# Attention with a routed expert layer: block table 0 emitted with preference, expert chunks let in earlier

## The chip, the cores and the metric

The kernel runs on one core of one Trainium2 chip. Its work is spread over TensorE (PE in the profile, with its weight loads as a row PEld of their own), VectorE (DVE), ScalarE (ACT), GpSimd (POOL) and the DMA queues, of which SyncE (SP) issues most. The metric is device time in microseconds (us) of one execution. Before the change three runs took 975.03, 975.57 and 981.8 us, with a median of 975.57 us; lower is better.

## The reference

An attention over 8 batches and 8 heads of 576 tokens and 64 dimensions, in which scores that are more than `tau` under the maximum of their row are left out, feeds a layer of 8 experts; each token goes to the one expert with the highest gate logit.

```python
scores = scale * np.matmul(q, k.transpose(0, 1, 3, 2))
thresh = np.max(scores, axis=-1, keepdims=True) - tau
scores = np.where(scores >= thresh, scores, -1000000000.0)
attn = np.exp(scores - np.max(scores, axis=-1, keepdims=True))
attn_out = np.matmul(attn / (np.sum(attn, axis=-1, keepdims=True) + 1e-09), v)
x = attn_out.transpose(0, 2, 1, 3).reshape(B * S, H * D)      # 4608 x 512
logits = x @ w_gate
expert_idx = np.argmax(logits, axis=1)
gate_w = softmax(logits)[np.arange(N), expert_idx]
for e in range(E):                                            # 8 experts
    mask = expert_idx == e
    out[mask] = gate_w[mask, None] * (np.maximum(x[mask] @ w1[e], 0.0) @ w2[e])
```

## The kernel before, in words

**Attention.** The 64 heads go in 32 pairs, 0 to 31, four pairs to a batch (called a block here, 0 to 7). The main loop goes through steps k, 11 to a pair; the attention's last step is 351 and `KEND` is 352. In a step the kernel emits one tile of `s` (scores from which DVE takes the row maxima, L358 to L370) for a pair ahead, and one tile of `st` (transposed scores less the threshold, L406 and L407) for the current pair. An `st` tile passes ACT (`exp`, L423) and DVE (mask, L426); of each two tiles ACT then makes an f16 copy `ph` (L431) and POOL the rest `pl` (L432). From `ph` and `pl` PE forms the product with the values (`av`, L476), some steps later. `st_30_1` is tile 1 of pair 30; `e_30_0`, `ph_30_0` and `pl_30_0` hold tiles 0 and 1 of it. Tiles `s`, `st`, `hi` and the experts' `h` all live in one pool of six PSUM banks (`ps_sc`).

**Routing.** When a block's four pairs are done, `finish` (L510) divides, splits and transposes its rows (transposes issued by SP, L552), `logits` (L560) forms gate logits `lg` on PE (L570), `route` (L585) takes the largest on DVE and ranks the tokens with a few matmuls `rk` (L621 to L624), and each token's row is sent to its expert's place in `xs` in DRAM (L644, POOL).

**Tables.** An expert's rows are read back in slots of 128. Which rows a slot holds stands in a table, made by `level` (L1018) from the counts (`pc`, L674) on DVE. Table 0 (`row0`, from `tables0`) is made after block 5 and serves slots 0 to 2, table 1 after block 6 and serves slots 3 to 6, table 2 after block 7 and serves the others. `fetch` (L830) gathers a slot's rows with POOL (L858, into `Rm`) and has SP transpose them into `xTm` (L868).

**Experts.** `gemm1` (L889, matmuls `h` of L913) and `gemm2` (L925, `y` of L946) are generators that hand their work over in chunks, 12 matmuls of 128 columns or the like each. The main loop lets chunks in by `RATE`: none before step `KM`, a fraction of a chunk a step from there to `KEND`, one a step after it.

**Order.** The order in which the program emits instructions is a preference. A scheduler places them on each engine by that preference and by when it expects operands and buffers to be ready; `hurry` (L181) marks what is emitted in it as preferred. Once placed, the order on each engine is fixed.

Of the kernel before, what the change touches and what calls it, by code (L numbers as in the profile page):

```python
# [26 lines left out]
EARLY = ((3, 0), (4, 3))  # L27
# [15 lines left out]
CAP = NTOK  # L43

TUNE = dict(
    lead=10, cast=2, sl=8, ll=15, sp0=3, sps=0, lv=-16, sv0=-6, sv1=2, av=2, g=4, l=3, d=4, g5=4, l5=3, d5=2, g6=1, l6=2, d6=2, g7=1, l7=1, d7=1, off=2, off5=1, off6=5, lg=4, lg7=6, km=16, rate=15, dh=1, do=3, ws0=6, wsd=2, w1d=5, plv=1, xv=5, so=0, sto=0, ord=0, sc=6, fa=3, fd=4, wa1=-70, wa2=-86, wl1=-28, wl2=-6, avb=1, route=1, ranks=7, pp=8, ew=4, maskat=0, w1a=-40, w1b=3,
)


# [1 line left out]
def kernel(  # L51
# [19 lines left out]
    ew = ctx.enter_context(tc.tile_pool(name="ew", bufs=4))  # L71
# [8 lines left out]
    pp = apool.enter_context(tc.tile_pool(name="pp", bufs=8))  # L80
# [100 lines left out]
    def hurry(f):  # L181

        def g():
            was, urgent[0] = urgent[0], True
            with tc.high_priority():
                f()
            urgent[0] = was

        return g

    def after(k, f, where=END):
        plan(now[0] + k, f, where)
# [479 lines left out]
    def counts(nm):  # L672
        pc = ps_m.tile([P, 512], F32, tag="m", name=f"pc_{nm}")
        nc.tensor.matmul(pc[:, 0:E], ones, run, start=True, stop=True)  # L674
        c = tp.tile([P, E], F32, name=f"cnt_{nm}")
        nc.vector.tensor_tensor(c, pc[:, 0:E], base_e, ALU.subtract)
        return c, pc

    def table_first(nm, bank, cnt, start=None):

        bc = [P, E, NE]
        if start is None:
            rk_i = tp.tile(bc, I32, name="rk_i")
            nc.gpsimd.iota(rk_i, pattern=[[0, E], [P, NE]], base=0, channel_multiplier=1)
            nc.vector.tensor_copy(rk_f, rk_i)
        rk, bad = (bank[:, z:z + E * NE].rearrange("p (e n) -> p e n", e=E) for z in (32, 96))
        if start is None:
            nc.scalar.copy(rk, rk_f)
        else:
            nc.vector.tensor_tensor(rk, rk_f, start.unsqueeze(2).to_broadcast(bc), ALU.add)  # L690
        lim = tp.tile([P, E, 1], F32, name=f"lim{nm}")
        nc.vector.scalar_tensor_tensor(lim[:, :, 0], bank[:, 0:E], -1.0, base_e, ALU.add, ALU.subtract)
        nc.vector.tensor_tensor(bad, rk, lim.to_broadcast(bc), ALU.is_gt)
        nc.vector.tensor_scalar(bad, bad, float(1 << 20), None, ALU.mult)
        badi = to_int(bad, bc, f"badi{nm}")
        nc.vector.tensor_tensor(rk, rk, lim.to_broadcast(bc), ALU.min)
        nc.vector.tensor_tensor(rk, rk, base_e.unsqueeze(2).to_broadcast(bc), ALU.add)

        has = tp.tile([P, E, 1], F32, name=f"has{nm}")
        nc.vector.scalar_tensor_tensor(has[:, :, 0], bank[:, 0:E], -0.5, base_e, ALU.add, ALU.is_gt)  # L700
        nc.vector.scalar_tensor_tensor(rk, rk, pos0, has.to_broadcast(bc), ALU.subtract, ALU.mult)
        nc.vector.tensor_scalar(rk, rk, pos0, None, ALU.add)
        rowi = to_int(rk, bc, f"row{nm}")
        return rowi, badi
# [81 lines left out]
    T = {}  # L786
# [231 lines left out]
    def level(nm, n, prev):  # L1018

        (cnt, bank), s_e, sp = counts(nm), None, None  # L1020
        if prev:

            nbe = tp.tile([P, E], F32, name=f"nbe{nm}")
            nc.vector.memset(nbe, 0.0)
            for e, i in enumerate(n[0]):
                if i:
                    nc.vector.memset(nbe[:, e:e + 1], float(i * P))
            s_e = tp.tile([P, E], F32, name=f"s_e{nm}")
            sp = bank[:, 16:16 + E]
            if prev[1] is None:  # L1030
                nc.scalar.copy(sp, prev[0])
                nc.vector.tensor_tensor(sp, sp, nbe, ALU.min)
            else:
                nc.scalar.copy(sp, prev[1])
                nc.vector.tensor_tensor(sp, sp, nbe, ALU.add)
                nc.vector.tensor_tensor(sp, sp, prev[0], ALU.min)
            nc.vector.tensor_tensor(sp, sp, nbe, ALU.subtract)
            nc.scalar.copy(s_e, sp)
        row, bad = table_first(nm, bank, cnt, sp)
        for e in range(E):  # L1040
            a, z = (x[e] if e < len(x) else 0 for x in n) if n[1] else (n[0][e] if e < len(n[0]) else 0, NE)
            for i in range(a, z):
                slots[NE * e + i] = row[:, e, i:i + 1], bad[:, e, i:i + 1], e % 2
                placed[NE * e + i] = B - 3 + int(nm)
        return cnt, s_e

    def tables0():
        T[0] = level("0", ((), EARLY[0]), None)
        for m in range(NF):
            after(1 + m, lambda m=m: fetch(m))  # L1050

# [44 lines left out]
    for i in range(8):  # L1096
        plan(k + WS0 + WSD * i, lambda i=i: split_w(*wseq[i]))
        if i + 2 < 8:
            plan(k + WS0 + WSD * i, lambda i=i: load_w(*wseq[i + 2]))
    TABLES = {B - 3: tables0, B - 2: tables1, B - 1: tables2}  # L1100
    plan(KEND + 12, close)

# [206 lines left out]
```

## Time and profile before

| what | value |
|---|---|
| median of the three runs | 975.57 us |
| the profiled execution's own time | 974.36 us |
| its span, first to last instruction | 972.6 us |
| PE busy | 932.8 us, 96% |
| PEld busy | 604.0 us, 62% |
| DVE busy | 696.2 us, 72% |
| ACT busy | 652.7 us, 67% |
| POOL busy | 559.0 us, 57% |
| HBM traffic | 90.24 MB read, 19.44 MB written |

Matmuls are pipelined: each row lasts until its result is out, while the next one starts long before that, so 96% of busy PE does not say that PE had no room. The shares are of the whole span; they change between the attention (to about 570 us, with three of the other engines near full) and the experts (from there on, with PE alone near full).

### The profile page before, as it was taken

Reading aid. Unit: us, or ns where it says so; the run is one execution under the profiler, and the core shown is the slowest. Engines: PE = TensorE matmul, PEld = TensorE weight load, DVE = VectorE, ACT = ScalarE, POOL = GpSimd, SP = SyncE. Lnnn points to the kernel's source line nnn. Section 1 sums busy time; section 2 is a strip of 40 time slices with the busy share of each in tenths; the row PEclk is TensorE's granted clock in tenths of the full one; section 3 lists DMA queues with packets and bytes.
Section 4 is the critical chain, followed back from the end, with each engine's and each line's share of the span. In section 5 each row is a group of like instructions: output and inputs, shape, how many; then the busy total and the mean of one; then the engine's idle time right before and its main releaser. Section 6 shows DMA issues by size and latency. Waiting matters only on the chain. (4 is left out here: it accounts for less than half of the span.)

```text
span 972.6 us, 28577 instructions
## 1 busy us (share of the span) xinstructions
PE 932.8 (96%) x11548; PEld 604.0 (62%) x11548; DVE 696.2 (72%) x1413; ACT 652.7 (67%) x1111; POOL 559.0 (57%) x467
## 2 busy tenths in 40 slices
PE   7899999999999999999997989999999999999997
PEld 2355555556556556565664677776677666677684
DVE  8899999999989999999999756835243341432650
ACT  2789898998988998989889944435333342433651
POOL 6466887897977998869979851531221212221121
PEclk9899999999999999999999999999999999999999
DMA  7642555474654674654647569998475565656720
GB/s 202 185 135 73 142 137 143 93 196 123 130 161 134 162 147 134 176 146 104 154 133 207 95 168 304 396 234 212 127 231 157 166 177 155 206 143 209 219 103 28
DMA packets 142707, 159.19 MB, mean 164 GB/s; under 512 B 96361, under 2 KB 112747, under 8 KB 142572
## 3 DMA queue, kind: packets, MB, share of 16 engines
q1 hardware_dynamic: 125782, 100.03, 41.1%
q10 hardware_dynamic: 7638, 27.85, 9.2%
q0 software_dynamic: 9152, 29.45, 8.9%
q8 instruction: 92, 1.51, 0.7%
q14 instruction: 43, 0.35, 0.1%
HBM read 90.24 MB, written 19.44 MB: 113 GB/s over the span
## 5 line engine op out<-in xcount | busy, mean ns | idle before, releaser
L432 POOL TENSOR_TENSOR pl<-e,ph 128x1024 f16<-128x1024 f32 x158 | 335.8, 2136 | 90.0 <-ACT ph L431 50.8
L423 ACT ACTIVATE e<-st,ntau 128x512 f32<-128x512 f32 (+1 forms) x352 | 222.2, 651 | 49.0 <-PE st L407 34.8
L426 DVE SCALAR_TENSOR_TENSOR e<-st,e 128x512 f32<-128x512 f32 (+1 forms) x352 | 219.1, 635 | 8.4 <-ACT e L423 7.8
L913 PEld LDWEIGHTS <-wb 128*128 128x128 f16 x2304 | 189.4, 98 | 20.3 <-DMA xTm<-Rm 1.3
L946 PE MATMUL y<-wb,hl 128*128 128x512 f16 (+1 forms) x1056 | 201.6, 360 | 0.0
L370 DVE TENSOR_REDUCE nm<-s 128x1 f32<-128x512 f32 x300 | 188.2, 631 | 14.7 <-PE s L360 13.4
L913 PE MATMUL h<-xTm,wb 128*128 128x256 f16 (+2 forms) x2112 | 196.3, 254 | 0.9 <-DVE lg L609 0.9
L476 PE MATMUL av<-vop,ph 128*128 128x65 f16 (+3 forms) x3072 | 187.7, 195 | 2.0 <-ACT x L486 1.2
L476 PEld LDWEIGHTS <-ph 128*128 128x128 f16 (+1 forms) x3072 | 157.8, 100 | 46.5 <-issue 17.0
L431 ACT CAST ph<-e 128x1024 f16<-128x1024 f32 x160 | 166.5, 1041 | 5.1 <-DVE e L426 4.5
L476 PE MATMUL av<-vop,pl 128*128 128x65 f16 (+1 forms) x1536 | 167.1, 194 | 2.1 <-POOL pl L432 1.6
L476 PEld LDWEIGHTS <-pl 128*128 128x128 f16 (+1 forms) x1536 | 135.7, 100 | 33.5 <-issue 9.8
L946 PEld LDWEIGHTS <-hl 128*128 128x128 f16 (+1 forms) x1056 | 94.1, 100 | 97.8 <-issue 1.9
L407 PE MATMUL st<-CQ,ck 128*128 128x512 f16 (+3 forms) x640 | 136.4, 287 | 4.6 <-DMA CQ<-ptT 3.0
L825 DVE SCALAR_TENSOR_TENSOR wb<-wf,wb 128x1024 f16<-128x1024 f32 x88 | 104.1, 1220 | 50.1 <-ACT wb L817 48.6
L406 PE MATMUL st<-QK 128*128 128x512 f16 (+3 forms) x640 | 138.0, 293 | 0.4 <-DVE nm L370 0.2
L358 PE MATMUL s<-QK 128*128 128x512 f16 (+1 forms) x600 | 129.0, 292 | 0.4 <-DVE nm L370 0.2
L960 POOL DMA_INDIRECT out_dram<-o,gt x40 | 46.5, 1163 | 141.2 <-ACT o L957 125.6
L360 PE MATMUL s<-ck,CQ 128*128 128x512 f16 (+1 forms) x600 | 127.1, 287 | 0.5 <-DMA CQ<-hi 0.5
L901 ACT ACTIVATE hl<-h 128x512 f16<-128x512 f32 (+1 forms) x80 | 45.8, 573 | 108.3 <-PE h L913 108.3
L817 ACT ACTIVATE wb<-wf 128x1024 f16<-128x1024 f32 x96 | 97.7, 1050 | 27.2 <-DMA wf<-in_w_dram 11.3
L871 DVE COPY gt<-R 128x1 f32<-128x1 f32 x33 | 5.1, 153 | 121.4 <-DMA out_dram<-o,gt 109.4
(193 smaller groups left out, 1002.4 us busy)
## 6 DMA issues: line engine op xcount, KB each, us to landing
wf<-in_w_dram SPq DMA_DIRECT2D x96, 512.0 KB
qkf<-in_qk_dram ACTq DMA_DIRECT2D x29, 576.0 KB
vf<-in_v_dram ACTq DMA_DIRECT2D x15, 640.0 KB
QK<-hi SPq DMA_DIRECT2D x62, 144.0 KB
QK<-lo SPq DMA_DIRECT2D x62, 72.0 KB
QK<-hi SPq DMA_DIRECT2D x62, 72.0 KB
ck<-lo SPq DMA_DIRECT2D x62, 72.0 KB
CQ<-hi SPq DMA_DIRECT2D x62, 64.0 KB
```

What stands on the lines that cost most here:

```text
L358: nc.tensor.matmul(sc[rows, oc], d["QA"][a][:, cols], d["KB"][a][:, CH[c]], start=True, stop=False)
L360: nc.tensor.matmul(sc[rows, oc], d["CQ"][:, at:at + cols.stop - cols.start], d["CK"][a][:, CH[c]], start=False, stop=True,)
L370: nc.vector.tensor_reduce(o, sc[:, 0:width(t)], axis=AX.X, op=ALU.max, negate=True)
L406: nc.tensor.matmul(sc[rows, oc], d["KB"][a][:, cols], d["QA"][a][:, CH[c]], start=True, stop=False)
L407: nc.tensor.matmul(sc[rows, oc], d["CK"][a][:, cols], d["CQ"][:, q], start=False, stop=True)
L423: nc.scalar.activation(pf, sc, AF.Exp, bias=ntau, scale=0.125 / SS)
L426: nc.vector.scalar_tensor_tensor(pf, sc, 0.0, pf, ALU.is_ge, ALU.mult)
L431: nc.scalar.copy(h, pd)
L432: (nc.vector if (n, t) in PLV else nc.gpsimd).tensor_tensor(l, pd, h, ALU.subtract)
L476: nc.tensor.matmul(av[:, 0:D] if z == 2 else av, l if z == 1 else h, vop[:, tv, W:W + D] if z == 2 else vop[:, tv, 0:W], start=i in (0, NT ...
L913: nc.tensor.matmul(o, Wt[:, c, wh, f], x, start=c == 0 and z == 0, stop=c == 3 and z == 2,)
L946: nc.tensor.matmul(o, h[:, hh], Wt[:, f, wh, c], start=f == 0 and z == 0, stop=f == 7 and z == 2)
```

## The change

Two edits. The first moves `km` from 16 to 26 and `rate` from 15 to 22, so that `RATE` lets chunks in from step 326 at 0.22 a step, and no longer from step 336 at 0.15. The second wraps the making of table 0 in `hurry`.

```diff
 TUNE = dict(
-    ..., lg=4, lg7=6, km=16, rate=15, dh=1, do=3, ...
+    ..., lg=4, lg7=6, km=26, rate=22, dh=1, do=3, ...
 )
 ...
     def tables0():
-        T[0] = level("0", ((), EARLY[0]), None)
+        hurry(lambda: T.__setitem__(0, level("0", ((), EARLY[0]), None)))()
         for m in range(NF):
             after(1 + m, lambda m=m: fetch(m))
```

By the running sum in the loop, chunks were emitted before `KEND` in steps 342 and 349; now they are in steps 330, 335, 339, 344 and 348. The instructions are the same ones in number and kind. What the scheduler makes of it differs in three places of importance.

**PE, at the start of pair 30.** Before, `st_30_1` followed the splits of a weight piece (`hi_w1_1`):

```order
L254 MATMUL hi_w1_1_0_12346<-wb2_0_11670,ident_h_99 128x512
...
L254 MATMUL hi_w1_1_1_12358<-wb2_0_11670,ident_h_99 128x512
...
L406 MATMUL st_30_1_12363<-QK_30_0_11141 128x512
...
L406 MATMUL st_30_2_12374<-QK_30_0_11141 128x512
...
L476 MATMUL av_29_0_12392<-vop_0_127,pl_29_8_12004 128x65
```

Now:

```order
L254 MATMUL hi_w1_1_1_12358<-wb2_0_11670,ident_h_99 128x512
...
L476 MATMUL av_29_0_12405<-vop_0_127,pl_29_8_12004 128x65
...
L381 MATMUL pst_31_12384<-ident_94,r_31_12344 9x128
...
L570 MATMUL lg_6_12495<-wg_107,xTg_6_0_12224 128x8
...
L476 MATMUL av_29_1_12613<-vop_0_127,pl_29_6_12204 128x65
...
L621 MATMUL rk_6_12832<-oh_6_12595,before_103 128x8
...
L913 MATMUL h_0_0_12363<-xTm_0_12227,wb1_0_11669 128x128
...
L406 MATMUL st_30_1_12376<-QK_30_0_11141 128x512
```

Ahead of `st_30_1` there are now the other 59 matmuls of `av_29_0`, all 90 of `av_29_1`, the logits `lg_6` (48), the ranks `rk_6` and the first 12 matmuls of `h_0_0`, slot 0's first expert product. Before, those came between or behind the `st` tiles of pairs 30 and 31; `h_0_0` began behind `st_31_1`.

**POOL, in the same stretch.** Before:

```order
L432 TENSOR_TENSOR pl_29_6_12204<-e_29_6_12202,ph_29_6_12203 128x1024
L432 TENSOR_TENSOR pl_30_0_12336<-e_30_0_12334,ph_30_0_12335 128x1024
L858 DMA Rm_0_12226<-xs_81,row0_12176 128x514
L858 DMA Rm_1_12273<-xs_81,row0_12176 128x514
L432 TENSOR_TENSOR pl_30_2_12379<-e_30_2_12377,ph_30_2_12378 128x1024
```

Now:

```order
L432 TENSOR_TENSOR pl_29_6_12204<-e_29_6_12202,ph_29_6_12203 128x1024
L858 DMA Rm_0_12226<-xs_81,row0_12176 128x514
L858 DMA Rm_1_12273<-xs_81,row0_12176 128x514
L876 TENSOR_TENSOR gt_0_0_12230<-Rm_0_12226,badi0_12168 128x1
L876 TENSOR_TENSOR gt_1_0_12277<-Rm_1_12273,badi0_12168 128x1
L858 DMA Rm_2_12351<-xs_81,row0_12176 128x514
L644 DMA xs_81<-R_129,posi_6_12599 36864x514
L876 TENSOR_TENSOR gt_2_0_12355<-Rm_2_12351,badi0_12168 128x1
L432 TENSOR_TENSOR pl_30_0_12336<-e_30_0_12334,ph_30_0_12335 128x1024
```

The gathers of slots 0 to 2 and one of the four sends of block 6 stand ahead of `pl_30_0` now; before, `pl_30_0` stood ahead of the first gather.

**SP, after the attention.** `spare` holds slots 3 and 4, `xTg_7` the transposed rows of block 7. Before:

```order
L802 DMA wf_1_0_0_13384<-in_w12_dram 128x1024
L868 DMA_TRANSPOSE spare_13231<-spare_13231 128x8x128 x2
L552 DMA_TRANSPOSE xTg_7_0_13426<-R_129 128x8x128 x2
L802 DMA wf_1_1_0_13441<-in_w12_dram 128x1024
L552 DMA_TRANSPOSE xTg_7_2_13445<-R_129 128x8x128 x2
```

Now:

```order
L802 DMA wf_1_0_0_13414<-in_w12_dram 128x1024
L868 DMA_TRANSPOSE spare_13271<-spare_13271 128x8x128 x2
L868 DMA_TRANSPOSE xTm_5_13615<-Rm_5_13614 128x8x128
L552 DMA_TRANSPOSE xTg_7_0_13435<-R_129 128x8x128 x2
L552 DMA_TRANSPOSE xTg_7_2_13454<-R_129 128x8x128 x2
```

The transpose of slot 5 (`xTm_5`) now stands ahead of those of block 7. On PE, the order between the end of the attention's last product (`av_31_1`) and the first logits of block 7 (`lg_7`) holds 5 matmuls of `h_1_1`, all 48 of `h_2_0`, `y_0` and 31 of `h_2_1`; before it held 32 of `h_1_1`, 36 of `h_2_0` and `y_0`.

## Rows read from the trace of the kernel before

**Rows 1.** The page's head and its first part: busy us, share, instructions.
```profile
span 972.6 us, 28577 instructions
PE 932.8 (96%) x11548; PEld 604.0 (62%) x11548; DVE 696.2 (72%) x1413; ACT 652.7 (67%) x1111; POOL 559.0 (57%) x467
```

**Rows 2.** Busy time by 10 us: stretch and length, engines, granted clock, DMA share, GB/s.
```profile
520.00:530.00 10.00, 7.10 (x58) 3.05 (x55) 10.00 (x22) 8.74 (x17) 9.61 (x10) 1.00 0.77 212
530.00:540.00 10.00, 7.15 (x117) 4.54 (x116) 7.96 (x21) 10.00 (x17) 9.84 (x7) 1.00 0.82 160
...
580.00:590.00 10.00, 8.09 (x125) 7.03 (x126) 4.18 (x7) 3.55 (x5) 1.49 (x2) 0.83 1.02 248
```

**Rows 3.** PE in order of time: start, us, operation, count [idle before, releaser].
```profile
530.77 0.38 PE L406 MATMUL st<-QK 128*128 128x512 f16 x1
...
531.63 0.19 PE L476 MATMUL av<-vop,pl 128*128 128x65 f16 x1
...
533.44 0.19 PE L476 MATMUL av<-vop,ph 128*128 128x64 f16 x1
...
546.88 1.07 PE L913 MATMUL h<-xTm,wb 128*128 128x128 f16 x16 [0.86 <-DVE lg L609]
...
559.02 3.52 PE L913 MATMUL h<-xTm,wb 128*128 128x128 f16 x60
...
581.91 0.46 PE L570 MATMUL lg<-wg,xTg 128*128 128x8 f16 x12 [3.02 <-DMA xTg<-R]
...
637.17 5.52 PE L913 MATMUL h<-xTm,wb 128*128 128x128 f16 x96
```

**Rows 4.** PE's weight loads in order of time, at the start of slot 0's product.
```profile
546.88 0.39 PEld L913 LDWEIGHTS <-wb 128*128 128x128 f16 x7 [1.35 <-DMA xTm<-Rm]
```

**Rows 5.** POOL in order of time, from 535 to 567 us.
```profile
535.48 4.21 POOL L432 TENSOR_TENSOR pl<-e,ph 128x1024 f16<-128x1024 f32 x2
539.85 1.01 POOL L858 DMA_INDIRECT Rm<-xs,row  x1 [0.16 <-PE hi_w L254]
...
565.99 0.99 POOL L644 DMA_INDIRECT xs<-R,posi  x1 [0.17 <-issue]
```

**Rows 6.** SP's DMA issues in order of time: start, us of issuing, count.
```profile
534.41 2.73 SPq L552 DMA_TRANSPOSE xTg<-R  x2
...
543.21 8.96 SPq L868 DMA_TRANSPOSE xTm<-Rm  x3
...
577.46 2.99 SPq L552 DMA_TRANSPOSE xTg<-R  x2
...
587.92 1.23 SPq L868 DMA_TRANSPOSE xTm<-Rm  x1
...
628.00 9.57 SPq L868 DMA_TRANSPOSE xTm<-R  x5
```

**Rows 7.** ACT in order of time, first and last of the attention's last two pairs.
```profile
531.79 0.69 ACT L423 ACTIVATE e<-st,ntau 128x512 f32<-128x512 f32 x1
...
561.04 1.04 ACT L431 CAST ph<-e 128x1024 f16<-128x1024 f32 x1
```

**Rows 8.** ACT's busy time from 531.8 to 562.1 us.
```profile
531.80:562.10 30.30, 28.91 (x53) 1.00 0.54 110
```

**Rows 9.** ACT's groups of that stretch: count | busy us, mean ns | idle before.
```profile
L431 ACT CAST ph<-e 128x1024 f16<-128x1024 f32 x11 | 11.6, 1054 | 0.4 <-DVE e L426 0.4
L817 ACT ACTIVATE wb<-wf 128x1024 f16<-128x1024 f32 x2 | 2.1, 1050 | 0.0
L486 ACT COPY x<-av 128x260 f32<-128x260 f32 x4 | 1.6, 396 | 0.3 <-PE av L476 0.3
L288 ACT ACTIVATE vop<-vf 128x640 f16<-128x640 f32 x1 | 0.7, 727 | 0.0
```

**Rows 10.** PE alone by 5 us, near the start: busy, granted clock, DMA share, GB/s.
```profile
30.00:35.00 5.00, 3.98 (x15) 0.61 0.69 192
```

**Rows 11.** POOL in order of time, near the start.
```profile
16.38 0.21 POOL L684 IOTA rk_i<- 128x32 int32 x1
```

More of the change, by code (lines that the diff above doesn't have):

```diff
@@ L45 @@
 TUNE = dict(
-    lead=10, cast=2, sl=8, ll=15, sp0=3, sps=0, lv=-16, sv0=-6, sv1=2, av=2, g=4, l=3, d=4, g5=4, l5=3, d5=2, g6=1, l6=2, d6=2, g7=1, l7=1, d7=1, off=2, off5=1, off6=5, lg=4, lg7=6, km=16, rate=15, dh=1, do=3, ws0=6, wsd=2, w1d=5, plv=1, xv=5, so=0, sto=0, ord=0, sc=6, fa=3, fd=4, wa1=-70, wa2=-86, wl1=-28, wl2=-6, avb=1, route=1, ranks=7, pp=8, ew=4, maskat=0, w1a=-40, w1b=3,
+    lead=10, cast=2, sl=8, ll=15, sp0=3, sps=0, lv=-16, sv0=-6, sv1=2, av=2, g=4, l=3, d=4, g5=4, l5=3, d5=2, g6=1, l6=2, d6=2, g7=1, l7=1, d7=1, off=2, off5=1, off6=5, lg=4, lg7=6, km=26, rate=22, dh=1, do=3, ws0=6, wsd=2, w1d=5, plv=1, xv=5, so=0, sto=0, ord=0, sc=6, fa=3, fd=4, wa1=-70, wa2=-86, wl1=-28, wl2=-6, avb=1, route=1, ranks=7, pp=8, ew=4, maskat=0, w1a=-40, w1b=3,
 )
```

## The prediction, made before the change was run

> **What bounds the kernel now.** The page's first part comes first [rows 1]: PE is busy for 96% of a span of 972.6 us. The profiled execution took 974.36 us, 1.76 more than its span and 1.21 less than the median of the three runs, 975.57; I sum against 974.36 and put the 1.21 back at the end. What a measurement of this kernel can tell from no change is about 1%, 9.8 us: under 965.8 is faster, over 985.3 slower.
>
> The whole span's share hides where there is room, so the windows come next [rows 2]. From 520 to 540 us, the end of the attention, PE is busy 7.10 and 7.15 of each 10 us while DVE, ACT and POOL stand at 7.96 to 10.00. The reader should see that PE waits there for its helpers. After the attention PE has one more gap: at 581.91 it had waited 3.02 us for the transposed rows of block 7 [rows 3], and its clock then fell from 2.4 to 1.2 GHz for part of 580 to 590, a mean grant of 0.83, which is 3.4 us at half speed, 1.7 us lost [rows 2]. Those two places are all that an earlier start of the experts can fill: 5.75 us in 520 to 540 and 3.0 + 1.7 behind it.
>
> **Chunks let in.** Sixty matmuls of 128 columns take 3.36 us, 0.056 us each (the row's 3.52 us from 559.02, less 0.16 by which the last outlasts its slot) [rows 3]; a chunk of 12 is 0.67 us. Five chunks instead of two before `KEND` could at most fill 3 x 0.67 = 2.0 us of PE's gaps. That is the gain in reach.
>
> **Table 0 with preference.** It can be ready earlier, but nothing waits for the table: the gather of slot 0 started at 539.85, right behind two `pl` on POOL that took 4.21 us [rows 5]. In the new order one of them (`pl_30_0`) stands behind the gathers, so the gather starts 2.1 us earlier, at 537.7. The index ramp `rk_i` and its cast move to the kernel's start, ahead of what the first matmuls need: one IOTA of 0.21 us [rows 11], at most 0.2 us late; I count 0.1.
>
> **The move that costs.** PE's rows of the trace start in the order in which the program places them. `st_30_1` started at 530.77 [rows 3] and now stands behind `av_29`, `lg_6`, `rk_6` and the first chunk of `h_0_0`. What does that wait for?
>
> 1. `h_0_0` had its operand last: PE's weight load stood 1.35 us until 546.88 for the transpose into `xTm` [rows 4]. From gather to use that chain took 546.88 - 539.85 = 7.0 us, with the transpose issued at 543.21 [rows 5, 6]. Started at 537.7 it ends at **544.8**.
> 2. The rest ahead of it is done sooner. 59 `av` matmuls started within 533.44 - 531.63 = 1.8 us [rows 3], 149 take 4.7. `lg_6` needs transposes issued from 534.41 on for 2.73 us [rows 6]; from issue to use 581.91 - 577.46 = 4.5 us is the longest that I find [rows 3, 6], so `lg_6` is over near 541, the 80 `av` behind it (2.5 us) and `rk_6` near 544.
> 3. The first chunk then takes 0.67 us, `st_30_1` starts at 545.5 and its exp on ACT at 546.1, against 531.79 [rows 7]: **14.3 us late**. In between ACT, DVE and POOL run dry, since no score tile comes.
> 4. ACT bounds the way back. From 531.8 to 562.1, when the last `ph` of the attention ended (561.04 + 1.04), it was busy 28.91 of 30.3 us [rows 7, 8]. Into the stall go one `ph` (1.05), two weight casts (2.1), two of four `x` copies (0.8) and the split of v (0.7) [rows 9]: 4.7 us. Left are 24.2 us if ACT never waits, 25.6 with its old 1.4 us of waits, and up to 1.3 more if the first casts stand behind masks. Some small pieces move ahead too, so I take 25.0 and keep 24.0 and 26.9 as ends. The last `ph` ends at 546.1 + 25.0 = 571.1, **9.0 us late**.
> 5. Behind that `ph` come POOL's `pl_31_6` and the last send of block 6 (565.99 [rows 5]); the gather of slots 3 and 4 waits for the sends, SP's transposes stand in a row behind that gather, and those of block 7 behind these (577.46). One send fewer stands there (I take 0.3 off), and the transpose of slot 5 is put ahead: one issue of 1.23 us [rows 6]. `lg_7` first starts 9.0 - 0.3 + 1.2 = **9.9 us late**, at 591.8.
> 6. PE has done more by then: 12 matmuls of `h_2_0` and 31 of `h_2_1`, 43 x 0.056 = 2.4 us. What is left after `lg_7` is so much less: 9.9 - 2.4 = **7.5 us late**. PE's gap ahead of `lg_7` is then some 2.5 us, near the old 3.02, so I let the slow clock come back as before; without it the sum is 5.8.
> 7. From there PE had no gap, and I see none made. The nearest is slot 7: its transpose was issued at 628.00, with 3.7 us to land as for `xTm` above it is there at 631.7, 5.5 ahead of its use at 637.17 [rows 3, 6]. Table 2 stands 65 matmuls of `h` and 4 of `y` later in PE's order, about 4.5 us, and 10 matmuls of `y` (2.2 us) were put ahead of the use; 3 us of slack stay.
>
> Sum: 0.1 + 7.5 = 7.6; 974.36 + 7.6 = 982.0 for a profiled run, 983.2 on the scale of the median. I forecast **983 us**, +0.8%. The bounds of step 4 (-1.0, +1.9), of the clock in step 6 (-1.7) and of step 1 (7.0 us of gather and transpose could be 1 us less, or more) make 979 to 987 of it.
>
> **Rivals.**
>
> *Interleaving pays (0.12).* PE's gaps of 520 to 540 are filled with three more chunks, 2.0 us, and the old waits stay: 975.57 - 2.0 = 973.6. For it speak those gaps [rows 2]; against it, that the chunk is put in front of the tiles on which the waiting engines live. The Trainium skill, Perfetto Trace Analysis, section Optimization Strategy, says that where the most contended engine changes over time, interleaving the regimes may gain. By that rule this is the result. The trace agrees with its premise and not, as I read the order, with its use here: a chunk fills a gap only if its operand is there, and this one lands 14 us after its place in the order.
>
> *The stall is paid once and regained (0.12).* If the attention's last tiles run faster than 25 us, since POOL and DVE start with nothing queued, and SP's new order does not hold `lg_7`, steps 5 and 6 shrink: ACT's 24.0 gives 8.0 late, less 2.4, less the slow clock 1.7, less the 1.2 of the transpose and the 0.3: about +2.4, 978. Against it: ACT cannot go under its own busy time [rows 8].
>
> *The clock stays low on the way back (0.20), slower.* In the stall PE idles: 4 us for `lg_6`'s transposes and some 1 to 2 for `xTm`, and after it PE has 20 score tiles less one at 0.43 us ((531.63 - 530.77) / 2 [rows 3]), 62 expert matmuls, 6 splits of 0.2 and 105 `av`: 8.2 + 3.5 + 1.2 + 3.3 = 16.2 us for ACT's 25. At 1.2 GHz that is 32.4, PE becomes the bound, and the attention ends 7.4 us later still: 983 + 7.4 = 990. It decides where the mean grant of that stretch falls under 16.2 / 25 = 0.65. For it: from 30 to 35 us the grant was 0.61 with PE busy 3.98 of 5 us [rows 10]. Against it: 7.1 of 10 us busy kept 1.00 from 520 to 540 [rows 2]. The Trainium skill, TensorE: Matmul & The Clock Gate, Part 1, says that the low clock is the default and that activity releases it. By that rule a stall that empties PE speaks against this change twice over; the rows show one fall after 3.02 us of idling, so it may cost 1.7 us rather than 7.4.
>
> **Chances.** The forecast's own case has 0.53, the rivals 0.12, 0.12 and 0.20, and 0.03 is left for what I do not see. Of the forecast's 979 to 987 about a quarter lies over 985.3, of the last rival nearly all: slower 0.33. Faster by over 1% needs more than the two gaps hold: 0.03. Within 1%: 0.64. The range is 975 to 989: it leaves out the first rival and the upper part of the last.
>
> **What would show it.** In the changed profile: a hole of some 14 us between two `e<-st` exps on ACT near 531 to 546; the gather of slot 0 near 537.7 and the first `h` near 544.8 (step 1); ACT's last `ph` near 571 (step 4); `lg_7` near 592 (step 5) with PE's wait ahead of it at 2 to 3 us; no gap later. I am wrong if the exps go on without a hole, if `lg_7` starts less than 5 us later than before, or if the grant stays under 0.7 from 545 to 570.

## The result, and the profile after

The changed kernel took 986.05 us in the median of six runs (985.72 to 987.46), the kernel before 975.30 us in six (973.68 to 981.80): a ratio of 1.0087, with a 95% interval of 1.0064 to 1.0111. The forecast was 983 us in a range of 975 to 989. The profiled execution took 986.27 us with a span of 984.5 us, 11.9 us more than that of before.

The page's head and its first part, of the changed kernel [rows 1]:

```profile
span 984.5 us, 28573 instructions
PE 938.6 (95%) x11548; PEld 605.9 (62%) x11548; DVE 696.3 (71%) x1413; ACT 651.9 (66%) x1111; POOL 556.9 (57%) x467
```

The windows of the changed kernel, with the columns of [rows 2]:

```profile
530.00:540.00 10.00, 5.71 (x138) 4.74 (x138) 4.63 (x18) 5.92 (x12) 9.19 (x7) 0.82 0.71 175
540.00:550.00 10.00, 7.76 (x108) 5.62 (x106) 3.48 (x14) 3.23 (x10) 2.51 (x5) 0.67 0.69 131
550.00:560.00 10.00, 9.21 (x90) 4.83 (x89) 9.16 (x26) 9.23 (x17) 6.87 (x5) 0.99 0.17 38
...
590.00:600.00 10.00, 7.31 (x82) 4.18 (x83) 4.11 (x8) 3.23 (x7) 1.20 (x2) 0.83 1.08 224
...
610.00:620.00 10.00, 6.99 (x98) 5.28 (x97) 6.67 (x12) 4.84 (x7) 1.15 (x1) 1.00 1.00 355
```

The work is the same, so the reader looks for the stretches in which nobody works. There are three. From 530 to 550 us ACT is busy for 9.15 of 20 us, where the kernel before kept it at 10.00 in the first ten [rows 2]. From 590 to 600 PE is busy 7.31. The last, 610 to 620 with 6.99, has no counterpart in the kernel before, where PE was fully busy:

```profile
610.00:620.00 10.00, 10.00 (x114) 7.17 (x112) 9.53 (x34) 7.38 (x11) 3.92 (x4) 1.00 1.03 413
```

**The first gap.** PE of the changed kernel in order of time [rows 3]: `h_0_0`, `st_30_1`, then block 7's `lg`, `rk` and table 2's `pc`:

```profile
545.65 0.83 PE L913 MATMUL h<-xTm,wb 128*128 128x128 f16 x12 [2.24 <-DMA xTm<-Rm]
546.31 0.38 PE L406 MATMUL st<-QK 128*128 128x512 f16 x1
...
592.69 0.46 PE L570 MATMUL lg<-wg,xTg 128*128 128x8 f16 x12 [3.37 <-DMA xTg<-R]
...
613.88 0.18 PE L621 MATMUL rk<-oh,before 128*128 128x8 f16 x1 [0.35 <-DVE run L613]
...
620.17 0.17 PE L674 MATMUL pc<-run,ones 128*128 128x8 f16 x1 [2.83 <-DVE posi L630]
```

ACT of the changed kernel [rows 7]: two exps that follow each other, a later one, and the attention's last `ph`; behind them ACT's window from the second exp to the end of that `ph` [rows 8]:

```profile
530.44 0.68 ACT L423 ACTIVATE e<-st,ntau 128x512 f32<-128x512 f32 x1
...
547.02 0.69 ACT L423 ACTIVATE e<-st,ntau 128x512 f32<-128x512 f32 x1 [2.81 <-PE st L407]
...
549.58 0.69 ACT L423 ACTIVATE e<-st,ntau 128x512 f32<-128x512 f32 x1 [0.96 <-PE st L407]
...
572.00 1.04 ACT L431 CAST ph<-e 128x1024 f16<-128x1024 f32 x1
```
```profile
547.00:573.10 26.10, 25.03 (x391) 17.78 (x390) 21.62 (x46) 24.11 (x42) 17.95 (x13) 0.94 0.15 43
```

`st_30_1` started 15.5 us later than before, right behind the first 12 matmuls of `h_0_0`, and those waited for slot 0's transpose. From the start of one exp to the start of the next 16.6 us passed (holes are counted so below, too). The idle time that the row names, 2.24 us, is only the end of the story: the score tile was held back through all that stands ahead of `h_0_0` as well. The way back then took 26 us, of which ACT was busy 24.1: ACT was its bound, but for 1.5 us in which it waited for score tiles of PE, 0.96 of them at 549.58.

**The late gap.** DVE of the changed kernel ahead of `pc_2`:

```profile
613.67 0.15 DVE L613 TENSOR_TENSOR run<-run,lg 128x8 f16<-128x8 f16 x1
616.76 2.50 DVE L825 SCALAR_TENSOR_TENSOR wb<-wf,wb 128x1024 f16<-128x1024 f32 x2 [2.94 <-ACT wb L817]
619.18 0.20 DVE L627 TENSOR_TENSOR rk<-rk,oh 128x40 f32<-128x40 f32 x1
...
619.92 0.20 DVE L630 TENSOR_REDUCE posi<-rk 128x5 int32<-128x40 f32 x1 [0.30 <-ACT sm L634]
```

The ranks' product `rk*oh` (L627) could have run at 614.5, when PE had finished `rk_7`. It stands behind two pieces of expert weights (L825), which wait for ACT's half of the split (L817), which waits for the piece's DMA. DVE idles 2.94 us, for most of which block 7's routing stands ready behind it, then works 2.50 us on the pieces. In `pc_2` PE waits for the result: its matmul needs only `run`, but shares a PSUM bank with `rk_7` (both come from `ps_m`, which has one), and `posi` is the last that reads that bank.

The pieces alone do not make the wait, since two of them stood there before, too. DVE of the kernel before:

```profile
597.11 1.23 DVE L825 SCALAR_TENSOR_TENSOR wb<-wf,wb 128x1024 f16<-128x1024 f32 x1 [1.55 <-ACT wb L817]
...
599.78 0.20 DVE L627 TENSOR_TENSOR rk<-rk,oh 128x40 f32<-128x40 f32 x1
...
601.72 0.19 DVE L630 TENSOR_REDUCE posi<-rk 128x5 int32<-128x40 f32 x1
```

From the end of `rk_7` to the end of `posi` DVE took 5.6 us then (596.28 to 601.91) and 5.6 us now (614.53 to 620.12). What changed is PE's work between `rk_7` and `pc_2`. Before, and then now:

```profile
596.14 3.51 PE L913 MATMUL h<-spare,wb 128*128 128x128 f16 x60
599.49 4.48 PE L946 MATMUL y<-wb,hl 128*128 128x512 f16 x20
603.80 0.17 PE L674 MATMUL pc<-run,ones 128*128 128x8 f16 x1
```
```profile
614.39 2.95 PE L913 MATMUL h<-spare,wb 128*128 128x128 f16 x50
```

It was 7.5 us and is 2.8; the rest of DVE's 5.6 us is PE's wait.

The experiments ran on other chips. The kernels of one set (e1 to e4, e5 to e8, e9 to e11, e12) shared a chip and the runs of the kernel before; in the first three sets that takes 990 to 992 us, and runs of one kernel there lie in two groups some 10 us apart, so a profiled execution can stand in another group than its median.

### The profile page after: what moved, and what is told of

Same layout as the page of the kernel before. It is cut to its first block, busy times and chain, and to the rows that moved or that the text cites. A ratio compares the mean times of both kernels' runs of the same rounds, so it can differ in the third digit from the quotient of the medians.

```text
span 984.5 us, 28573 instructions
## 1 busy us (share of the span) xinstructions
PE 938.6 (95%) x11548; PEld 605.9 (62%) x11548; DVE 696.3 (71%) x1413; ACT 651.9 (66%) x1111; POOL 556.9 (57%) x467
## 5 line engine op out<-in xcount | busy, mean ns | idle before, releaser
L370 DVE TENSOR_REDUCE nm<-s 128x1 f32<-128x512 f32 x300 | 188.1, 631 | 14.3 <-PE s L360 13.1
L825 DVE SCALAR_TENSOR_TENSOR wb<-wf,wb 128x1024 f16<-128x1024 f32 x88 | 103.9, 1220 | 55.5 <-ACT wb L817 55.3
L817 ACT ACTIVATE wb<-wf 128x1024 f16<-128x1024 f32 x96 | 97.8, 1049 | 29.8 <-DMA wf<-in_w_dram 13.6
```

The source lines that it names most:

```text
L370: nc.vector.tensor_reduce(o, sc[:, 0:width(t)], axis=AX.X, op=ALU.max, negate=True)
```

## The experiments

The theory, called queue theory in the expectations: the banks of `ps_sc` are handed out in the order in which the program asks for them. `h_0_0` asks in step 330, between `st_30_0` and `st_30_1`; until it can use its bank, no later tile gets one. The rivals: the preference for table 0, the number of chunks as such, PE's own line.

**e1 and e2: the two edits apart.** e1 is the changed kernel with

```diff
-    km=26, rate=22
+    km=16, rate=15
```

> Table 0 with preference, but km=16 and rate=15 as before. PE, ACT and SP have the order of before; only some small pieces of the kernel's start move on DVE and POOL. Queue theory (the loss comes from the first chunk's place, since the score tiles asked for behind it wait for it): 975.3 us give or take 1, the exps go on without a hole, gather of slot 0 near 539.8. Rival (the preference for table 0 has a share in the loss): 978 or more.

e2 is the kernel before with `km=26, rate=22`.

> km=26 and rate=22, table 0 as before the change. Queue theory: all of the loss is here, 986 us give or take 1, the hole in ACT's exps 15 us long, last ph near 573. Rival (the preference has a share): under 984.

e1 took 990.64 us against 991.50 of the kernel before: 0.9992, interval 0.9953 to 1.0032. e2 took 994.15: 1.0046, 1.0006 to 1.0086. e2 has the hole (14.7 us), e1 none. ACT of e2:

```profile
534.80 0.68 ACT L423 ACTIVATE e<-st,ntau 128x512 f32<-128x512 f32 x1
...
549.46 0.69 ACT L423 ACTIVATE e<-st,ntau 128x512 f32<-128x512 f32 x1 [0.50 <-PE st L407]
```

The preference for table 0 shows no effect clear of the noise; the hole is the chunks'. But on this chip the loss is 3 us in the medians and not 11: the expected times of both were missed, and e11 looks at why. The profiled executions differ by more: e1's, one of its two shortest, has a span of 980.0 us and e2's 991.8, and `lg_7` starts at 587.32 and 593.93.

**e3: the operand there from the start.**

```diff
                         x = xT[:, 2 * c + xh] if late(g[0]) else xT[:, 0:n, 2 * c + xh]
+                        if (g[0], u) == (0, 0):
+                            x = ones.unsqueeze(1)
```

> The changed kernel, but the first 48 matmuls of slot 0 (h_0_0) multiply a tile of ones that is there from the start instead of slot 0's gathered rows, so their place in the order stays early and their wait goes; a quarter of slot 0's first product is thereby another. Queue theory: h_0_0 goes right behind st_30_0, st_30_1 follows near 532.5, no hole over 2 us between exps, last ph near 562, lg_7 within 2 us of 582, time 973 to 977. If early chunks pay at all, it is here: up to 2.0 us under 975.3. Rival (the chunks' number and the weights, transposes and casts that move with them cost by themselves): the waits of PE near 617 stay, 3 us, and the time is 977.5 to 980.

It took 983.92 us, 0.9912 of the kernel before (0.9879 to 0.9944) and 10.2 us under e2. PE of e3, `st_30_0` to `st_30_1`:

```profile
532.16 0.61 PE L406 MATMUL st<-QK 128*128 128x512 f16 x1
...
535.74 3.30 PE L915 MATMUL h<-ones,wb 128*128 128x128 f16 x31
538.87 0.38 PE L406 MATMUL st<-QK 128*128 128x512 f16 x1
```

The chunk is asked for in the same early step, and more of it stands ahead of `st_30_1` (31 matmuls for 12), yet the hole is gone: no gap between exps over 6.0 us, for 6.1 in e1. The 2 us expected are less than e1 shows, too. `st_30_1` is still 3.2 us later than e1's (535.64), but `lg_7` only 2.1. So the wait of the first chunk makes the hole, and not the number of chunks. The time shows less than the trace: of the 10.2 us, 4.5 stand at `lg_7` in the profiled executions (589.41 for 593.93), and from there to 700 us PE's mean granted clock was 0.98 for e2's 0.94, where no chunk was changed. The gain is more than the 2.0 us expected at most, against a kernel before that loses time of its own on this chip (e11). PE's wait at `pc_2` did not go altogether: it was 1.3 us.

**e5 and e6: the same wait, another bank.** e5 gives `h_0_0` a bank apart, and leaves five to the pool; e6 has five and none apart.

```diff
-    sc=6
+    sc=5
```
```diff
+    ps_h = ctx.enter_context(tc.tile_pool(name="ps_h", bufs=1, space=bass.MemoryType.PSUM))
...
-            ph = ps_sc.tile(...)
+            ph = (ps_h if (g[0], u) == (0, 0) else ps_sc).tile(...)
```

> The changed kernel, but h_0_0 has a PSUM bank of its own and the tiles of ps_sc share five banks instead of six. The first chunk is emitted at the same step and waits for slot 0's rows as in the changed kernel; only the place of its bank is another. Queue theory (the score tiles wait because banks of one pool are handed out in the order asked for): st_30_1 follows st_30_0 within 5 us, no hole over 8 us between exps after 525, h_0_0 starts near 545 to 549 behind st_30_7, and the time is 9 us or more under that of the run with five banks and no bank apart. Rival (it is the wait of h_0_0 in PE's own line, wherever its bank is): a hole of 10 us or more stays and the two five-bank runs are within 3 us of each other.

> The changed kernel with five banks in ps_sc instead of six and none apart: the control of the run with a bank apart. Queue theory: st_30_1 stands behind h_0_0 as in the changed kernel, hole in the exps 15 to 18 us, the time that of the changed kernel on the same chip or up to 5 us more for the missing bank. Rival (with five banks the score tiles run otherwise and the hole shrinks): hole under 10 us.

PE of e5, `st_30_0`, `st_30_1` and the first matmuls of `h_0_0` (its lines are one further down):

```profile
549.06 0.38 PE L407 MATMUL st<-QK 128*128 128x512 f16 x1
...
551.17 0.38 PE L407 MATMUL st<-QK 128*128 128x512 f16 x1
...
567.78 1.39 PE L914 MATMUL h<-xTm,wb 128*128 128x128 f16 x22 [1.41 <-DMA xTm<-Rm]
```

PE of e6, the same three in their new order:

```profile
544.69 0.38 PE L406 MATMUL st<-QK 128*128 128x512 f16 x1
...
561.00 0.83 PE L913 MATMUL h<-xTm,wb 128*128 128x128 f16 x12
561.67 0.38 PE L406 MATMUL st<-QK 128*128 128x512 f16 x1
```

In e5 `h_0_0` still waits for its rows, until 567.78 (the 545 to 549 expected left out that with five banks all of this stands some 20 us later), and `st_30_1` follows `st_30_0` by 2.1 us; in e6 by 17.0 us. The longest time without an exp is 5.8 against 14.6 us, and e5 took 1002.62 us (1.0117 of the kernel before, 1.0067 to 1.0167), e6 1010.64 (1.0193, 1.0147 to 1.0239): 8.0 us less, where 9 or more were expected. With a bank of its own `h_0_0` is placed behind the score tiles, and they do not wait for it: the order in which banks are asked for makes the queue, and PE's line follows it. A bank apart is no remedy, since five banks cost more than the hole: e6 took 16.5 us more than the changed kernel with six (e8), where up to 5 were expected.

**e4, e9, e10: the first chunk later.** `km=20, rate=22` (step 336), `km=16, rate=22` (step 340), `km=16, rate=30` (step 339, four chunks), all with the preference for table 0.

> km=20 and rate=22 with the preference for table 0: the first chunk in step 336 instead of 330, one chunk fewer ahead of the attention's end. Queue theory: st_30_4 is the first tile behind h_0_0; it started at 540.58 before and cannot start ahead of 546, so the hole in the exps is 5 to 6 us long, the last ph about 4 us late (566), the time 978 to 980. Rival (a loss by chunks let in early, whatever stands behind them): four of five chunks keep four fifths of the loss, 984.

> km=16 and rate=22 with the preference for table 0: the first chunk in step 340, three chunks ahead of the attention's end instead of two before and five in the change. Queue theory: st_31_0 is the first tile behind h_0_0; it would start within 3 us of its old place, no hole over 7 us between exps, last ph within 2 us of the kernel before on the same chip, and the time within 2 us of it (one chunk more in PE's gaps is worth 0.7 us at most). Rival (any chunk more ahead of the end costs its share, 11 us over three chunks): 3 to 4 us over the kernel before.

> km=16 and rate=30 with the preference for table 0: four chunks ahead of the attention's end, the first in step 339. Queue theory: st_30_7 is the first tile behind h_0_0, 3 to 4 us later than before, the last ph 1 to 3 us late, time 1 to 3 us over the kernel before. If filling PE's gaps with chunks pays more than that, the time is under the kernel before by up to 1.3 us. Rival (each chunk more costs its share): 7 us over.

ACT of e4 has its hole later and shorter, from 546.78 to 554.77, 8.0 us where 5 to 6 were expected (the first row groups two exps, the second of which starts at 546.78):

```profile
546.57 0.89 ACT L423 ACTIVATE e<-st,ntau 128x64 f32<-128x64 f32 x2 [1.39 <-PE st L407]
...
554.77 1.46 ACT L423 ACTIVATE e<-st,ntau 128x512 f32<-128x512 f32 x2 [1.77 <-PE st L407]
```

Its last `ph` is 3.8 us later than e1's, as expected. e9 and e10 have no gap over 5.8 us, and their last `ph` stands at 567, a microsecond ahead of e11's. So the hole follows the place of the first chunk as the theory has it. The times do not: e4 took 997.95 us (1.0067, 1.0030 to 1.0104), more than e2 with its longer hole; e9 995.65 (1.0092, 1.0057 to 1.0127); e10 985.81 (0.9952, 0.9924 to 0.9981), the only kernel with the whole of the work whose interval lies under the one before. What comes behind `lg_7` parts e4 from e10: from there to the end their profiled executions took 404.8 and 393.9 us. e9's is the shortest of its eleven, 982.87 us, so why its median is 5.6 us over the kernel before, with no hole, is not shown; that more chunks cost something of their own is not excluded by it.

**e7 and e8: the late gap.** e8 is the changed kernel again; e7 takes expert 1's low halves from DVE to POOL:

```diff
+        if e == 1:
+            nc.gpsimd.tensor_tensor(o[:, :, 1], x, o[:, :, 0], ALU.subtract)
+        else:
-        nc.vector.scalar_tensor_tensor(...)
+            nc.vector.scalar_tensor_tensor(...)
```

> The changed kernel, but the eight low halves of expert 1's weight pieces are formed on POOL instead of DVE (by a subtraction without the scale, so expert 1's low halves hold other numbers). It leaves the hole alone and takes the pieces that wait for the DMA out of DVE's line, in which block 7's routing stands. Theory (of the 11.9 us lost, some 3 are PE's waits for block 7's ranks and counts, which stand on DVE behind weight pieces that have not landed): the waits of PE at rk_7 and pc_2, 0.4 and 2.8 us, go, and the time is 2 to 4 us under that of the changed kernel on the same chip. Rival (the weights themselves are what is late): the wait moves to the products h_4 to h_6 of expert 1 or to slot 7, and the time stays within 1.5 us.

> The changed kernel unaltered, beside the three others on their chip: 11 us over the kernel before where that runs near 975; a hole of 15 to 17 us in the exps, waits of PE at lg_7 and near pc_2.

PE's waits from 590 to 660 us (us in all, times, longest), of e8 and then of e7:

```profile
PE pc L674 <- DVE posi L630: 4.1, 1, 4.1
PE lg L570 <- DMA xTg<-R: 3.3, 1, 3.3
```
```profile
PE lg L570 <- DMA xTg<-R: 3.5, 1, 3.5
PE h L916 <- issue: 2.4, 3, 1.0
```

DVE's way from the end of `rk_7` to that of `posi` fell from 6.8 to 2.7 us (PE's order left 4.5 us of work beside it, for 2.8 in e8). The wait at `pc_2` went (at `rk_7` e8 had none), `pc_2` ran at 612.38 and not at 623.21, and the time fell from 994.13 to 990.17 us (0.9998 of the kernel before, 0.9965 to 1.0032; e8 1.0047, 1.0019 to 1.0075): 4.0 us, in the range expected. e8's own ratio is short of the expected 11 us, like e2's.

**e11: the kernel before on such a chip.**

> The kernel before unaltered, for a profile on the chip of these runs: where it takes 990 us and not 975, the profile shows which stretch the extra time is in. Theory (pieces of expert 1's weights and block 7's routing behind them come late on such a chip, as they do in the changed kernel): waits of PE between 595 and 660 us, 5 us or more in all. Rival (the extra time lies in the attention ahead of 530 us): st_30_0 10 us later than 528.4 and no such waits.

It took 993.49 us, 1.0030 of itself (0.9982 to 1.0077), which shows how far two series of one kernel stand apart there. PE's waits from 590 to 660 us of its profiled execution, 995.42 us:

```profile
PE h L913 <- issue: 5.7, 9, 1.2
PE rk L621 <- DVE run L613: 1.7, 1, 1.7
```

Its `st_30_0` is 4.5 us late against the first chip (532.82 for 528.37), `lg_7` 7.4, the first matmul of slot 7 21.0 (658.21 for 637.17 [rows 3]), and the end no more than that. So 13.6 of the 21.0 us arise behind `lg_7`, over half of them as these waits. Another 3.3 us are the clock's, which was short of full speed by 1.6 to 1.7 us in each of three windows, and before in one [rows 2]:

```profile
600.00:610.00 10.00, 8.28 (x120) 7.79 (x119) 7.18 (x14) 5.29 (x8) 1.30 (x1) 0.83 1.03 300
...
620.00:630.00 10.00, 8.45 (x50) 4.15 (x48) 7.71 (x26) 5.39 (x7) 1.00 (x1) 0.83 1.01 379
...
640.00:650.00 10.00, 10.00 (x85) 5.97 (x83) 2.01 (x10) 1.36 (x3) 1.42 (x4) 0.84 0.89 158
```

The waits are as long as the theory had them, but only the one at `rk_7` is shown to be of its kind. For those at `h` the profile names nothing that PE waited for ("issue"), and six of the nine, 3.9 us, end from 634.75 to 639.78, when neither ACT nor DVE forms a piece of weights. No such wait stands in either profile of the first chip; what it is stays open. The attention's part, 4.5 to 7.4 us, is the rival's, smaller than it had it. So why the same hole costs less here in the medians is not shown. What goes with the longer times is the clock: from `lg_7` to 700 us the mean grant was 0.98 to 1.00 in the profiled executions under 987 us (e1, e3, e9, e10) and 0.92 to 0.95 in those of 990 us and more with six banks (e2, e4, e7, e8, e11).

**e12: both losses avoided.** e10's settings, and expert 1's low halves formed off DVE:

```diff
+        if e == 1:
+            nc.scalar.activation(x, x, AF.Copy, scale=SW)
+            nc.gpsimd.tensor_tensor(o[:, :, 1], x, o[:, :, 0], ALU.subtract)
```

> km=16 and rate=30 (four chunks, the first in step 339), and expert 1's low halves formed off DVE: ACT scales the piece in place, POOL subtracts. Both losses that the runs named are avoided: few score tiles stand behind the first chunk, and block 7's routing has no weight piece ahead of it on DVE. Theory: the four-chunk run's ratio of 0.995 and the 4 us that the halves on POOL gave add up: 0.990 to 0.994 of the kernel before, no wait of PE at rk_7 or pc_2 over 1 us. Rival (the pieces of expert 1 and 2 are late whoever forms them, and ACT's eight extra passes make them later): 0.995 or more, with PE waiting at h_4 to h_7.

On a chip where the kernel before takes 977.34 us it took 977.97: 1.0015, 1.0002 to 1.0028. The theory's gain of 0.6 to 1% did not come; the time is the rival's, without the waits that it named. `lg_7` started 4.2 us later than in [rows 3] after a wait of 3.7 us for an expert's `hl`, `h_0_0` waited 2.8 us for `xTm`, and `pc_2` still 1.3 us, now because `posi` on DVE stood behind ACT, which had eight more passes in its line:

```profile
602.85 0.20 DVE L630 TENSOR_REDUCE posi<-rk 128x5 int32<-128x40 f32 x1 [3.90 <-ACT sm L634]
```

So no version here was shown to beat the kernel before on more than one chip.

## Why the prediction came out as it did

The mechanism was the one forecast up to step 6. By the steps, in profiled executions:

| step | forecast | measured |
|---|---|---|
| 1: `h_0_0` starts | 544.8 | 545.65 |
| 2: `rk_6` done | near 544 | 543.41 |
| 3: exp of `st_30_1` | 14.3 late | 15.2 late |
| 4: last `ph` ends | 571.1, 9.0 late | 573.04, 11.0 late |
| 5: `lg_7` starts | 591.8, 9.9 late | 592.69, 10.8 late |
| 6: wait ahead of it; slow clock behind it | 2.5; yes | 3.37; yes |
| 7: gaps made behind it | none | 0.35 + 2.83 |

Steps 1 to 3 held within a microsecond. In step 1 the gather was right (537.39 for 537.7), and gather to use took 8.3 us for the 7.0 of [rows 4, 5]. I put the earlier gather down to where `pl_30_0` stands, and that holds, but it has nothing to do with the preference: e1, which has the preference alone, keeps the old order. Step 4 was 1 us short on the way back: ACT's work was as forecast (24.1 us busy, against 24.2), its waits were 2.0 us and not 0.8, the longest the 0.96 us at 549.58 for a tile that PE formed at the low clock. Step 5 gave some of that back: from the last `ph` to `lg_7` it was 19.7 us, before 19.8, so that SP's extra transpose did not show.

**Step 7 failed.** "From there PE had no gap, and I see none made": two were made, 3.2 us together. I looked at the rows of slot 7 and found their slack, and counted that table 2 stands 65 matmuls of `h` and 4 of `y` later in PE's order. I did not count that `rk_7`, whose bank its `pc_2` waits for, stands 75 of `h` and 24 of `y` later: PE's work between the two fell from 7.5 to 2.8 us, against 5.6 us that DVE takes from one to the other, weight pieces included. With `lg_7` at +10.8, less the credit of 2.4 that I counted in step 6, plus 3.2, the sum is 11.6 of the 11.9 us measured; with step 7 as forecast it would have been 8.4, near the 7.6. e7 shows on another chip that the wait at `pc_2` goes, and 4.0 us with it, when the pieces leave DVE. That the median lies within 975 to 989 all the same is owed to the room left for other steps, and in that to luck.

**The rivals.** *Interleaving pays* did not happen, for the reason given. The Trainium skill, Perfetto Trace Analysis, section Optimization Strategy, says that interleaving regimes may help where the most contended engine changes. No run here shows such a gain by itself: e3 is under the kernel before by its median, but its profiled execution reaches `lg_7` 2.1 us after e1's. What e2 and e3 show is a condition: the chunk's operand has to be there when its turn for a bank comes. *The stall is paid once and regained* falls with the row of ACT, which could not go faster than its own work. *The clock stays low on the way back* was to decide at a mean grant under 0.65: from 547.0 to 573.1 it was 0.94. The clock did fall in the hole, with 0.65 to 0.67 in each 5 us from 535 to 550, the matmuls of `st_30_2` 0.43 us apart as at 1.2 GHz, and stood at 0.99, all but 2.4 GHz, from 550 to 555. The Trainium skill, TensorE: Matmul & The Clock Gate, Part 1, says that the low clock is the default and activity releases it: this trace agrees. Its price here was about 1 us, the wait of ACT at 549.58; from 550 on ACT and not PE bounded the stretch.

## What to carry to other kernels

Where tiles of two loops share a pool, ask first in which order they ask for their buffers: one request whose operand is late holds up every request behind it, however ready these are, so the first chunk of the new loop should ask no earlier than its data lands. When a stretch is pushed back, look at how much work each engine still has between the two ends of a short chain through another engine, and not only at the slack of the next big transfer. A size measured on one chip need not be that of another: this change cost 11 us where the kernel before takes 975 us, and its chunks, or all of it, about 3 us on two chips where it takes 991.

## What the runs showed of the hardware that was not expected

An instruction on DVE can take several times its usual time beside POOL. In e7 one piece of weights on DVE, 1.2 us elsewhere, lasted from 611.97 to 617.14, while POOL ran three subtractions of the same size until 616.05. DVE of e7, then POOL:

```profile
611.97 5.17 DVE L828 SCALAR_TENSOR_TENSOR wb<-wf,wb 128x1024 f16<-128x1024 f32 x1 [1.27 <-ACT wb L817]
```
```profile
609.73 6.32 POOL L826 TENSOR_TENSOR wb<-wf,wb 128x1024 f16<-128x1024 f32 x3
```

It ended 1.09 us after POOL's last, as if it had waited for POOL and then run. e12, the other run with such subtractions on POOL, has one of 7.84 us. DVE of e12, then POOL:

```profile
614.47 7.84 DVE L829 SCALAR_TENSOR_TENSOR wb<-wf,wb 128x1024 f16<-128x1024 f32 x1
```
```profile
614.93 6.30 POOL L827 TENSOR_TENSOR wb<-wf,wb 128x1024 f16<-128x1024 f32 x3
```

It ended 1.08 us after POOL's last. Two short instructions, elsewhere under 0.2 us, were stretched as well, to 4.76 us in e7 (from 623.18) and 2.82 us in e12 (from 605.15), and both ended with POOL's pieces. In e8, with no piece on POOL, none of the 88 on DVE lasted over 1.23 us. The Trainium skill, Trainium Architecture — The Big Picture, section What this means for kernel authors, says that the port which the two share is an exclusive lock. These four instructions agree. Not every instruction of DVE is held, though: in e7 seven from 604.34 to 605.96, of 0.16 to 0.23 us, ran at their usual length inside POOL's two pieces of 604.32 to 608.55. Which are held no run here shows.
